# Four load buffers that keep their columns of ones, and a running maximum, in an attention and expert kernel

## The chip, the cores and the metric

The kernel runs on one core of a Trainium2 chip. The metric is the device time of one execution in microseconds (us). The engines are called PE (matrix products; PEld is its weight load), DVE, ACT, POOL and SP; SP issues the plain transfers, POOL the scatters.

## What is computed

```python
B, N, C = (4, 11456, 128); n_agents = 49
def sm(a, b):
    s = scale * (a @ b.transpose(0, 2, 1))
    s = s - s.max(-1, keepdims=True)
    e = np.exp(s)
    return e / (e.sum(-1, keepdims=True) + 1e-09)
a2k = sm(agents, k)
agent_v = a2k @ v
q2a = sm(q, agents)
attn = q2a @ agent_v                 # 4 x 11456 x 128
# then, with the 45824 rows as x, an expert layer with 8 experts:
logits = x @ w_gate
expert_idx = np.argmax(logits, axis=1)
probs = softmax(logits)
h = np.maximum(x_sorted[lo:hi] @ w1[e], 0.0)
y_sorted[lo:hi] = h @ w2[e]          # rows sorted by expert
out = gate_w[:, None] * y
```

The agents look at the keys of their batch with a softmax over 11456 keys, so the maximum and the sum run over all keys. Each query row then looks at 49 agents, is sent to one expert, and is weighted by its gate.

## The kernel before

A batch has 90 blocks of 128 rows. Keys and values are worked off in nine units of ten blocks (UB = 10, 640 KB each); queries in units of eight or ten. For the keys (`k_ops`) a unit is loaded to a buffer of the ring `cf` (L357), ACT rounds it to f16 (`chi`, L361), DVE makes the rest (`clo`, L365), PE forms the scores in PSUM (L380 to L382), ACT copies them to `S` (L425), and DVE takes the maximum of the unit's ten blocks (L430), one column of `mx` for each unit. After the ninth, DVE reduces `mx` (L439), and a short chain over PE, DVE and ACT spreads the maximum `m`. For the values (`v_ops`) POOL first writes a column of ones behind each of the ten blocks of a `cf` buffer (L485), SP loads the ten blocks between them (L488), DVE or POOL subtracts `m` (L491), ACT takes the exponential (L494), and PE sums `S` times `v` and, by the ones, the softmax's denominator (L502). ACT copies the two halves of the sum to `vsum` (L517).

`cf` has four buffers, which keys, values, most of the queries and four of the w2 experts share in turn. A buffer is handed on when its last readers are done.

The expert part sorts a group's rows by expert (`r_ops`, on DVE), scatters them to DRAM with one POOL transfer for each block (`rows`, L951), and reads them back as tiles of 128 rows of one expert. A tile is two layers on PE (L1020 and L1021, then L1027, L1028 and L1033), a relu on ACT (L1069), its f16 rest on DVE (`hlo`, L1073), a scaling on ACT (`yo`, L1084) and a scatter of the rows by POOL (`out`, L951). There are 372 tiles in nine groups; the first group has only 16 blocks, so that tiles begin early. Keys, values and queries of later batches are worked off between tiles. On each engine the order of instructions is fixed when the program is built: a planner (`Plan.run`) simulates the engines with a cost for each step and a key that says when it is due, and emits the steps in the order in which its simulation starts them. A step's cost in the planner thus changes the order of all that comes later.

Of the kernel before, what the change touches and what calls it, by code (L numbers as in the profile page):

```python
# [11 lines left out]
F32 = mybir.dt.float32  # L12
# [12 lines left out]
A = 49  # L25
# [194 lines left out]
def agent_attention_moe(ctx: ExitStack, tc: tile.TileContext, qT, kT, v, agT, wg, w1, w2, out):  # L220
    nc = tc.nc
# [12 lines left out]
    def buf(name, shape, dt=F32, **kw):  # L234
        return wk.tile(shape, dt, name=name, bufs=RINGS.get(name, 1), **kw)
# [56 lines left out]
    PL = Plan()  # L292
# [4 lines left out]
    def dve(n):  # L297
        return 0.07 + 0.00104 * n
# [45 lines left out]
    def dma(src, dst, nbytes, key, deps=(), new=(), use=(), q=None, fn=None):  # L344
        return PL.op("SP", 0.53, fn or (lambda: nc.sync.dma_start(dst(), src())), key, deps,
                     new=new, use=use, nbytes=nbytes)


    def split(src, key, hk, pool=False, ring="cf", ub=UB):

        st = Rec()
        n = ub * P
        gf, gh, gl = Gen(ring), Gen("chi"), Gen("clo")

        def ld():
            st.f = buf(ring, [P, UB * (P + 1)] if ring == "cf" else [P, F])[:, :n]
            nc.sync.dma_start(st.f, src)  # L357

        def hi():
            st.hi = buf("chi", [P, UC], F16)[:, :n]  # L360
            nc.scalar.copy(st.hi, st.f)  # L361

        def lo():
            st.lo = buf("clo", [P, UC], F16)[:, :n]
            (nc.gpsimd if pool else nc.vector).tensor_sub(st.lo, st.f, st.hi)  # L365
        o0 = dma(None, None, P * n * 4, key, new=[gf], fn=ld)
        st.ld = o0
        o1 = PL.op("ACT", 0.03 + act(n), hi, hk, [o0], new=[gh], use=[gf])
        o2 = PL.op("POOL" if pool else "DVE", pol(n) if pool else dve(n), lo, hk, [o1], new=[gl], use=[gf, gh])
        return st, [o1, o2], [gh, gl]  # L370
# [33 lines left out]
    def k_ops(t, key, pool=()):  # L404

        b = t.b
        agents_ops(t, key())
        t.gS, t.gmx = Gen("S"), Gen("mx")
        t.o_s = []

        def begin():
            t.S = buf("S", [P, NBLK, A])
            t.mx = buf("mx", [P, NU, A])
            nc.gpsimd.memset(spacer, 0.0)
        ob = PL.op("POOL", 0.04, begin, key(), new=[t.gS, t.gmx])
        om = []
        for u in range(NU):
            k = key()
            st, sp, gs = split(kT[b][:, u * UC:(u + 1) * UC], k - 1.5, k, pool=u in pool)
            r, o, gm = scores(t, st, sp + [ob], gs, k)  # L420
            t.ga.users.append(o)
            sl = slice(u * UB, (u + 1) * UB)

            def cp(sl=sl, r=r):
                nc.scalar.copy(t.S[:, sl], r.p)  # L425

            def mx(sl=sl, u=u):
                if u == NU - 1:
                    nc.vector.memset(t.S[TAIL:, NBLK - 1], NEG)
                nc.vector.tensor_reduce(t.mx[:, u], t.S[:, sl].rearrange("p k a -> p a k"), axis=AX.X, op=OP.max)  # L430
            o = PL.op("ACT", act(UA), cp, k, [o, ob], use=[gm, t.gS])
            o = PL.op("DVE", 0.9, mx, k, [o], use=[t.gS, t.gmx])
            t.o_s.append(o)
            om.append(o)
        t.gm, g1 = Gen("m"), Gen("m1")

        def red():
            t.m1 = buf("m1", [P, A])
            nc.vector.tensor_reduce(t.m1, t.mx.rearrange("p u a -> p a u"), axis=AX.X, op=OP.max)  # L439


        x = Rec()
        g2, g3, gp, gq = Gen("mt"), Gen("mg"), Gen("misc"), Gen("misc")

        def tr():
            x.p = misc([A, P])
            nc.tensor.transpose(x.p, t.m1, identf)

        def diag():
            x.t = buf("mt", [A, 1])  # L450
            nc.vector.tensor_reduce(x.t, x.p, axis=AX.X, op=OP.max)
            x.d = buf("mg", [A, A])
            nc.vector.tensor_scalar(x.d, identf[:A, :A], x.t, None, op0=OP.mult)

        def every():
            x.q = misc([P, A])
            nc.tensor.matmul(x.q, onesf[:A], x.d, start=True, stop=True)

        def cpm():
            t.m = buf("m", [P, A])  # L460
            nc.scalar.copy(t.m, x.q)
        k = key()
        o = PL.op("DVE", dve(NU * A), red, k, om, new=[g1], use=[t.gmx])
        o = PL.op("PE", 0.25, tr, k, [o], new=[gp], use=[g1])
        o = PL.op("DVE", 0.4, diag, k, [o], new=[g2, g3], use=[gp])
        o = PL.op("PE", 0.25, every, k, [o], new=[gq], use=[g3])
        t.o_m = PL.op("ACT", act(A), cpm, k, [o], new=[t.gm], use=[gq])

    def v_ops(t, key, pool=()):

        b = t.b
# [4 lines left out]
        for u in range(NU):  # L476
            en, ec, ew = ("POOL", pol, nc.gpsimd) if u in pool else ("DVE", dve, nc.vector)
            k = key()
            sl = slice(u * UB, (u + 1) * UB)
            st = Rec()  # L480
            gf = Gen("cf")

            def one(st=st):
                st.f = buf("cf", [P, UB, P + 1])
                nc.gpsimd.memset(st.f[:, :, P:], 1.0)  # L485

            def ld(u=u, st=st):
                nc.sync.dma_start(st.f[:, :, 0:P], v[b][:, u * UC:(u + 1) * UC].rearrange("p (k c) -> p k c", c=P))  # L488

            def sub(sl=sl, ew=ew):  # L490
                ew.tensor_tensor(t.S[:, sl], t.S[:, sl], t.m[:, None, :].to_broadcast([P, UB, A]), op=OP.subtract)  # L491

            def ex(sl=sl):
                nc.scalar.activation(t.S[:, sl], t.S[:, sl], AF.Exp, scale=scale)  # L494

            def mm(u=u, st=st):

                if u == 0:
                    r.v = misc([P, P + 1])
                for j in range(UB):  # L500
                    h = 64 * (j % 2)
                    nc.tensor.matmul(r.v[h:h + A], t.S[:, u * UB + j], st.f[:, j], start=(u == 0 and j < 2),  # L502
                                     stop=(u == NU - 1 and j >= UB - 2))
            o = PL.op("POOL", 0.14, one, k - 1.5, new=[gf])
            ol = dma(None, None, P * UC * 4, k - 1.5, [o], use=[gf], fn=ld)
            t.o_vl.append(ol)
            o = PL.op(en, ec(UA), sub, k, [t.o_m] + t.o_s[u:u + 1], use=[t.gS, t.gm])
            o = PL.op("ACT", act(UA), ex, k, [o], use=[t.gS])
            oM.append(PL.op("PE", UB * 0.087, mm, k, [o, ol] + oM[-1:], new=[] if u else [gv],
                            use=[gf, t.gS] + ([gv] if u else [])))  # L510

# [2 lines left out]
        t.gav, t.gab, t.gan, t.gG, t.gbm = Gen("av"), Gen("ab"), Gen("an"), Gen("G"), Gen("bm")  # L514

        def c0(h):
            nc.scalar.copy(vsum[h:h + A], r.v[h:h + A])  # L517

        def c1():
            r.l = misc([P, 1])  # L520
# [16 lines left out]
            t.ab = buf("ab", [P, A])  # L537
            nc.vector.scalar_tensor_tensor(t.ab, t.av[:, A2:A2 + A], -1.0, t.av[:, A2:A2 + A], op0=OP.mult, op1=OP.max)
        k = key()
        o = [PL.op("ACT", 0.17, lambda h=h: c0(h), k, oM, use=[gv]) for h in (0, 64)]  # L540
        o = PL.op("PE", 0.1, c1, k, o + [o_cst], new=[gm])
        o = PL.op("DVE", 0.5, c1b, k, [o], new=[g1, gs], use=[gm])
        o = PL.op("PE", 0.22, c1c, k, [o], new=[ga], use=[gs])
# [558 lines left out]
    def w_ops(e, lkey, key):  # L1102

        r = Rec()
        ring = "S" if e in W2S else "cf" if e in W2CF else "wf"
        t = BT[0]
        gf = t.gS if ring == "S" else Gen(ring)

        def ld():
            if ring == "S":  # L1110
                i = len(W1S) + W2S.index(e)
                r.f = t.S.rearrange("p k a -> p (k a)")[:, i * F:(i + 1) * F]
            else:
                r.f = buf("cf", [P, UB * (P + 1)])[:, :F] if ring == "cf" else buf("wf", [P, F])
            nc.sync.dma_start(r.f, w2[e])
            r.f = r.f.rearrange("p (k d) -> p k d", d=P)

        def hi():
            m = w2s[:, e].rearrange("p (k i d) -> p k i d", i=2, d=P)
            r.hi, r.lo = m[:, :, 0], m[:, :, 1]  # L1120
            nc.scalar.activation(r.hi, r.f, AF.Copy, scale=SW)

        def lo():
            nc.vector.scalar_tensor_tensor(r.lo, r.f, SW, r.hi, op0=OP.mult, op1=OP.subtract)

# [137 lines left out]
```

## Time and profile before

| | |
|---|---|
| time, median of 3 runs | 1520.91 us (1517.16 to 1523.62) |
| the profiled execution: its time, its span | 1521.53 us, 1519.7 us |
| busy: PE, DVE, POOL, ACT | 1180.8, 860.7, 834.2, 753.3 us |
| mean busy share of the 16 DMA engines on SP's queue | 37.9% |

The span is the time from the first to the last instruction; the rest of the 1521.53 us lies around it. A busy PE counts pipelined matmuls, so it isn't PE at its peak.

### The profile page before, as it was taken

To read this page: it belongs to the slowest core of one execution; us is meant where nothing else is said; L and a number is where in the kernel's file an instruction comes from. 1 tells how busy PE (TensorE), PEld (TensorE's weight loads), DVE (VectorE), ACT (ScalarE), POOL (GpSimd) and SP (SyncE) were. 2 spreads that over 40 slices of the span, in tenths; PEclk is the share of its full clock that TensorE was granted. 3 is DMA by queue.
4 is the path that set the end of the run, shared out by engine and by line. 5 is a ranking of instruction groups with operands and counts; after the bars stand their busy time and mean duration, and the time that the engine had idled before them with its cause. 6 is when DMAs were issued, how large, how long until landed. Compare 5 with 4: busy or idle time off the path is not lost. (4 is left out here: it accounts for less than half of the span.)

```text
span 1519.7 us, 46051 instructions
## 1 busy us (share of the span) xinstructions
PE 1180.8 (78%) x18670; PEld 1066.0 (70%) x18670; DVE 860.7 (57%) x1273; ACT 753.3 (50%) x1162; POOL 834.2 (55%) x1537
## 2 busy tenths in 40 slices
PE   4743767778877798888777788888787887879995
PEld 3442666567777786767777786777777776779995
DVE  7674675367657646574557754568447433334553
ACT  5552734354644545554554544646454443435663
POOL 1156355655556656566556755556556555664443
PEclk9866778999889998999899989999999999999998
DMA  8988435764174377264252639346131123132220
GB/s 281 322 281 237 129 97 165 203 214 105 29 220 121 109 189 224 69 176 134 60 177 71 179 83 287 87 120 152 38 100 40 41 78 108 41 66 71 49 47 23
DMA packets 222099, 198.40 MB, mean 131 GB/s; under 512 B 121123, under 2 KB 189869, under 8 KB 221857
## 3 DMA queue, kind: packets, MB, share of 16 engines
q1 hardware_dynamic: 198432, 162.15, 37.9%
q0 software_dynamic: 23424, 33.05, 7.7%
q8 instruction: 149, 2.44, 0.7%
q14 instruction: 94, 0.76, 0.2%
HBM read 107.98 MB, written 59.60 MB: 110 GB/s over the span
## 5 line engine op out<-in xcount | busy, mean ns | idle before, releaser
L1073 DVE SCALAR_TENSOR_TENSOR hlo<-hp,hhi 128x1024 f16<-128x1024 f32 x372 | 452.8, 1222 | 448.3 <-ACT hhi L1069 403.0
L951 POOL DMA_INDIRECT out<-yo,rt x372 | 388.8, 1045 | 501.2 <-ACT yo L1084 470.1
L1069 ACT ACTIVATE hhi<-hp 128x1024 f16<-128x1024 f32 x372 | 380.8, 1024 | 253.5 <-PE hp L1021 115.8
L1027 PE MATMUL yp<-Wst,hhi 128*128 128x128 f16 x2976 | 394.3, 225 | 118.8 <-ACT yo L1084 96.5
L951 POOL DMA_INDIRECT rows<-rows,idx x360 | 376.8, 1047 | 118.4 <-issue 82.5
L1020 PE MATMUL hp<-ec,Mst 98*128 98x128 f16 x2976 | 407.4, 226 | 29.4 <-issue 16.5
L1021 PE MATMUL hp<-ec,Mst 98*128 98x128 f16 x2976 | 405.1, 226 | 16.6 <-issue 15.9
L1028 PE MATMUL yp<-Wst,hhi 128*128 128x128 f16 x2976 | 394.3, 225 | 3.7 <-issue 3.7
L1028 PEld LDWEIGHTS <-hhi 128*128 128x128 f16 x2976 | 300.4, 101 | 131.7 <-issue 130.6
L1020 PEld LDWEIGHTS <-Mst 98*128 98x128 f16 x2976 | 300.7, 101 | 40.4 <-issue 31.1
L1021 PEld LDWEIGHTS <-Mst 98*128 98x128 f16 x2976 | 301.6, 102 | 28.7 <-issue 27.9
L1027 PEld LDWEIGHTS <-hhi 128*128 128x128 f16 x2976 | 299.8, 101 | 23.7 <-issue 15.7
L1084 ACT ACTIVATE yo<-yp,rt 128x128 f32<-128x128 f32 x372 | 137.0, 368 | 301.3 <-PE hp L1021 175.4
L1033 PE MATMUL yp<-Wst,hlo 128*128 128x128 f16 x2976 | 246.0, 226 | 28.3 <-issue 15.4
L1033 PEld LDWEIGHTS <-hlo 128*128 128x128 f16 x2976 | 191.0, 102 | 47.3 <-issue 25.2
L382 PE MATMUL misc<-a,clo 128*128 128x49 f16 x720 | 79.1, 194 | 42.7 <-issue 26.3
L365 DVE TENSOR_TENSOR clo<-cf,chi 128x1280 f16<-128x1280 f32 (+1 forms) x71 | 104.6, 1473 | 10.4 <-ACT chi L361 6.5
L361 ACT CAST chi<-cf 128x1280 f16<-128x1280 f32 (+1 forms) x71 | 88.7, 1251 | 35.4 <-remote 13.2
L380 PE MATMUL misc<-a,chi 128*128 128x49 f16 x720 | 78.7, 194 | 32.5 <-ACT chi L361 18.8
L382 PEld LDWEIGHTS <-clo 128*128 128x128 f16 x720 | 65.5, 103 | 43.0 <-issue 25.0
L380 PEld LDWEIGHTS <-chi 128*128 128x128 f16 x720 | 66.6, 103 | 40.1 <-ACT chi L361 19.9
L381 PE MATMUL misc<-a,chi 128*128 128x49 f16 x720 | 78.8, 195 | 14.7 <-issue 14.6
(173 smaller groups left out, 955.7 us busy)
## 6 DMA issues: line engine op xcount, KB each, us to landing
cf<-in_kT SPq DMA_DIRECT2D x36, 640.0 KB
cf<-in_v SPq DMA_DIRECT2D x36, 640.0 KB
cf<-in_qT SPq DMA_DIRECT2D x32, 640.0 KB
Mst<-md SPq DMA_DIRECT2D x30, 512.0 KB
Wst<-w2s SPq DMA_DIRECT2D x30, 512.0 KB
wf<-in_w SPq DMA_DIRECT2D x28, 512.0 KB
rows<-padrow SPq DMA_DIRECT2D x4, 2304.0 KB
md<-mm SPq DMA_DIRECT2D x56, 128.0 KB
```

The source lines that it names most:

```text
L365: (nc.gpsimd if pool else nc.vector).tensor_sub(st.lo, st.f, st.hi)
L380: nc.tensor.matmul(p[:, j], h, t.a[:, 0], start=True, stop=False)
L382: nc.tensor.matmul(p[:, j], l, t.a[:, 0], start=False, stop=True)
L951: st = nc.gpsimd.indirect_dma_start(out=dst, out_offset=bass.IndirectOffsetOnAxis(ap=idx, axis=0), in_=src, in_offset=None, **kw)
L1020: nc.tensor.matmul(h_, m[:A2, h, c:c + P], e, start=True, stop=False)
L1021: nc.tensor.matmul(h_, m[:A2, h, 512 + c:512 + c + P], e, start=False, stop=True)
L1027: nc.tensor.matmul(yp, h, w[:, fb * 256 + P:(fb + 1) * 256], start=(fb == 0), stop=False)
L1028: nc.tensor.matmul(yp, h, w[:, fb * 256:fb * 256 + P], start=False, stop=False)
L1033: nc.tensor.matmul(yp, lo[:, fb * P:(fb + 1) * P], w[:, fb * 256:fb * 256 + P], start=False, stop=(fb == FB - 1))
L1069: nc.scalar.activation(x.hi, x.hp, AF.Relu)
L1073: nc.vector.scalar_tensor_tensor(x.lo, x.hp, 0.0, x.hi, op0=OP.max, op1=OP.subtract)
L1084: nc.scalar.activation(x.yo, x.yp, AF.Copy, scale=r.rt[:, o, 1:2].bitcast(F32))
```

## The change

Four buffers `CF` are now made once, with columns of ones that are written at the start and never again: a column of ones, then two blocks of 128, then a column of ones, and so on. The first block of a pair has its ones on its left, the second on its right. All loads to `cf` (keys, values, queries, w2) go between the columns, in pieces of two blocks: 1024 bytes. Before, those of v were pieces of 512 bytes, and those of keys and queries 5120 (4096 for units of eight blocks and for w2). The nine POOL writes of ones for each batch are gone. For the maximum, DVE keeps a running maximum of 128x490 over the units (nothing for the first unit, the first against the second for the second), and the last reduce takes the ten blocks of it. The copy of the first half of the sum is two ACT instructions, since its ones stand on the other side.

```diff
+    PW = 2 * P + 1
+    CF = [cst.tile([P, UB // 2 * PW + 1], F32, name=f"cf{i}") for i in range(RINGS["cf"])]
+    for t in CF:
+        nc.gpsimd.memset(t[:, 0::PW], 1.0)
+    cf_n = [0]
+
+    def cfbuf():
+        cf_n[0] += 1
+        return CF[(cf_n[0] - 1) % len(CF)]
+
+    def pairs(t, n):
+
+        return t[:, 1:1 + n // 2 * PW].rearrange("p (s c) -> p s c", c=PW)[:, :, 0:2 * P]
...
-            st.f = buf(ring, [P, UB * (P + 1)] if ring == "cf" else [P, F])[:, :n]
-            nc.sync.dma_start(st.f, src)
+            st.f = pairs(cfbuf(), ub) if ring == "cf" else by_pairs(buf(ring, [P, F])[:, :n])
+            nc.sync.dma_start(st.f, by_pairs(src))
...
-            t.mx = buf("mx", [P, NU, A])
+            t.mx = buf("mx", [P, UB, A])
...
-                nc.vector.tensor_reduce(t.mx[:, u], t.S[:, sl].rearrange("p k a -> p a k"), axis=AX.X, op=OP.max)
+                nc.vector.tensor_tensor(t.mx, t.S[:, 0:UB] if u == 1 else t.mx, t.S[:, sl], op=OP.max)
             o = PL.op("ACT", act(UA), cp, k, [o, ob], use=[gm, t.gS])
-            o = PL.op("DVE", 0.9, mx, k, [o], use=[t.gS, t.gmx])
+            if u:
+                o = PL.op("DVE", dve(UA), mx, k, [o] + t.o_s[-1:], use=[t.gS, t.gmx])
...
-            def one(st=st):
-                st.f = buf("cf", [P, UB, P + 1])
-                nc.gpsimd.memset(st.f[:, :, P:], 1.0)
-
             def ld(u=u, st=st):
-                nc.sync.dma_start(st.f[:, :, 0:P], v[b][:, u * UC:(u + 1) * UC].rearrange("p (k c) -> p k c", c=P))
+                st.f = cfbuf()
+                nc.sync.dma_start(pairs(st.f, UB), by_pairs(v[b][:, u * UC:(u + 1) * UC]))
...
-            o = PL.op("POOL", 0.14, one, k - 1.5, new=[gf])
-            ol = dma(None, None, P * UC * 4, k - 1.5, [o], use=[gf], fn=ld)
+            ol = dma(None, None, P * UC * 4, k - 1.5, new=[gf], fn=ld)
...
-            nc.scalar.copy(vsum[h:h + A], r.v[h:h + A])
+            if h:
+                nc.scalar.copy(vsum[h:h + A], r.v[h:h + A])
+            else:
+                nc.scalar.copy(vsum[0:A, P:], r.v[0:A, 0:1])
+                nc.scalar.copy(vsum[0:A, 0:P], r.v[0:A, 1:])
```

On SP, the loads of v for the first batch (L488) stood so, with the semaphores that each waits for:

```order
L488 DMA cf<-in_v 128x10x128 [waits DMAHW0_49,DVE_49]
L488 DMA cf<-in_v 128x10x128 [waits DMAHW1_49,DVE_49]
L488 DMA cf<-in_v 128x10x128 [waits DMAHW2_49,DVE_49]
L357 DMA wf<-in_qT 128x1024 x2
L488 DMA cf<-in_v 128x10x128 [waits DMAHW3_49,PE_49,Pool_49]
L488 DMA cf<-in_v 128x10x128 [waits DMAHW5_49,PE_49,Pool_49]
L488 DMA cf<-in_v 128x10x128 [waits DMAHW4_49,DMAHW6_49,PE_49,Pool_49]
L488 DMA cf<-in_v 128x10x128 [waits DMAHW7_49,PE_49,Pool_49]
L488 DMA cf<-in_v 128x10x128 [waits DMAHW2_49,PE_49,Pool_49]
```

With the change the same loads are L505, and stand in the same order:

```order
L505 DMA cf_111<-in_v 128x5x256 [waits DMAHW0_49,DVE_49]
L505 DMA cf_112<-in_v 128x5x256 [waits DMAHW1_49,DVE_49]
L505 DMA cf_109<-in_v 128x5x256 [waits DMAHW2_49,DVE_49]
L376 DMA wf<-in_qT 128x1024 x2
L505 DMA cf_110<-in_v 128x5x256 [waits DMAHW3_49,PE_49]
L505 DMA cf_111<-in_v 128x5x256 [waits DMAHW5_49,PE_49]
L505 DMA cf_112<-in_v 128x5x256 [waits DMAHW6_49,DMAHW4_49,PE_49]
L505 DMA cf_109<-in_v 128x5x256 [waits DMAHW7_49,PE_49]
L505 DMA cf_110<-in_v 128x5x256 [waits DMAHW2_49,PE_49]
```

Nothing moved here; the last five no longer wait for POOL, only for PE, which frees the buffer. In exchange the first four loads of keys, which waited for nothing, now wait for POOL's writes of ones.

On DVE, where the keys of the second batch begin among the first tiles (L365 is `clo`, L1073 `hlo` of a tile, L430 the maximum, L723 and L724 belong to the queries), the rows were:

```order
L687 TENSOR_TENSOR rows<-ef,rows 128x10x49
L1073 SCALAR_TENSOR_TENSOR hlo<-hp,hhi 128x1024
L365 TENSOR_TENSOR clo<-cf,chi 128x1280
L1002 UNCONDITIONAL_BRANCH
L1073 SCALAR_TENSOR_TENSOR hlo<-hp,hhi 128x1024
L430 TENSOR_REDUCE mx<-S 128x49
L1002 UNCONDITIONAL_BRANCH
L365 TENSOR_TENSOR clo<-cf,chi 128x1280
L723 TENSOR_TENSOR lg<-ls 128x80
```

Now they are (L384 for L365, L1094 for L1073):

```order
L708 TENSOR_TENSOR rows<-ef,rows 128x10x49
L1094 SCALAR_TENSOR_TENSOR hlo<-hp,hhi 128x1024
L384 TENSOR_TENSOR clo<-cf_112,chi 128x1280
L1023 UNCONDITIONAL_BRANCH
L1094 SCALAR_TENSOR_TENSOR hlo<-hp,hhi 128x1024
L1023 UNCONDITIONAL_BRANCH
L384 TENSOR_TENSOR clo<-cf_109,chi 128x1280
L744 TENSOR_TENSOR lg<-ls 128x80
```

The maximum of the first unit has gone from this place; the next one stands behind the sorting of a group's rows in both.

On DVE again, the keys of the third batch (units two to five) were spread among tiles so:

```order
L1073 SCALAR_TENSOR_TENSOR hlo<-hp,hhi 128x1024 x2
L430 TENSOR_REDUCE mx<-S 128x49
L1002 UNCONDITIONAL_BRANCH
L365 TENSOR_TENSOR clo<-cf,chi 128x1280
L1002 UNCONDITIONAL_BRANCH
L1073 SCALAR_TENSOR_TENSOR hlo<-hp,hhi 128x1024 x2
L430 TENSOR_REDUCE mx<-S 128x49
L1002 UNCONDITIONAL_BRANCH
L365 TENSOR_TENSOR clo<-cf,chi 128x1280
L1002 UNCONDITIONAL_BRANCH
L1073 SCALAR_TENSOR_TENSOR hlo<-hp,hhi 128x1024 x2
```

Now the maxima of the second to fourth unit (L449) stand so:

```order
L449 TENSOR_TENSOR mx<-S 128x490
L384 TENSOR_TENSOR clo<-cf_109,chi 128x1280
L449 TENSOR_TENSOR mx<-mx,S 128x490
L1094 SCALAR_TENSOR_TENSOR hlo<-hp,hhi 128x1024
L1023 UNCONDITIONAL_BRANCH
L384 TENSOR_TENSOR clo<-cf_110,chi 128x1280
L449 TENSOR_TENSOR mx<-mx,S 128x490
L1094 SCALAR_TENSOR_TENSOR hlo<-hp,hhi 128x1024
L1023 UNCONDITIONAL_BRANCH
L1094 SCALAR_TENSOR_TENSOR hlo<-hp,hhi 128x1024
L449 TENSOR_TENSOR mx<-mx,S 128x490
```

Counted by the rows of L1073, the nine maxima of this batch lay between the 72nd and the 85th tile, and the eight lie now between the 79th and the 86th; those of the last batch lay between the 158th and the 173rd, and lie now between the 164th and the 177th.

## Rows read from the trace of the kernel before

**Rows 1.** Busy time by engine in two stretches, then clock, DMA share, GB/s.

```profile
0.00:160.00 160.00, 75.20 (x1027) 59.52 (x1028) 100.54 (x216) 69.41 (x105) 63.72 (x121) 0.77 0.84 267
160.00:1368.00 1208.00, 971.72 (x15272) 873.51 (x15271) 687.56 (x997) 601.33 (x938) 704.81 (x1292) 0.94 0.45 123
```

**Rows 2.** Waits over the whole run: us in total, times, longest.

```profile
PE yp L1027 <- ACT yo L1084: 96.5, 117, 3.1
...
POOL cf L485 <- PE misc L502: 13.9, 8, 5.0
...
PE yp L1033 <- DVE hlo L1073: 12.7, 10, 6.2
...
ACT chi L361 <- DMA cf<-in_qT: 6.7, 4, 3.4
...
PE misc L502 <- DMA cf<-in_v: 5.0, 6, 1.4
```

**Rows 3.** Timeline, PE, first batch's values: start, length, count, idle before.

```profile
35.42 7.35 PE L502 MATMUL misc<-cf,S 128*49 128x129 f32 x80 [1.69 <-issue]
...
44.03 1.31 PE L502 MATMUL misc<-cf,S 128*49 128x129 f32 x20
...
53.35 1.31 PE L502 MATMUL misc<-cf,S 128*49 128x129 f32 x20 [1.09 <-DMA cf<-in_v]
```

**Rows 4.** Timeline, SP and POOL, around the fifth and ninth load of v.

```profile
37.88 0.38 SPq L488 DMA_DIRECT2D cf<-in_v  x1
...
45.42 1.92 SPq L488 DMA_DIRECT2D cf<-in_v  x1
...
34.05 4.61 POOL L491 TENSOR_TENSOR S<-S,m 128x490 f32<-128x490 f32 x3 [6.25 <-ACT m L461]
38.61 0.11 POOL L485 MEMSET cf<- 128x10 f32 x1
```

**Rows 5.** As rows 1, while v is loaded and while w1 and w2 are.

```profile
40.00:50.00 10.00, 7.69 (x147) 7.01 (x144) 6.40 (x8) 4.58 (x9) 2.12 (x6) 1.00 0.97 265
56.00:66.00 10.00, 6.08 (x42) 2.89 (x43) 6.83 (x36) 4.00 (x10) 0.00 (x0) 0.61 1.02 413
```

**Rows 6.** Timeline, SP and POOL, the first microseconds.

```profile
1.69 1.38 SPq L357 DMA_DIRECT2D cf<-in_kT  x3
...
2.50 0.10 POOL L414 MEMSET spacer<- 1x1 f32 x1
```

**Rows 7.** Timeline, ACT and DVE, the first batch's keys.

```profile
6.07 1.26 ACT L361 CAST chi<-cf 128x1280 f16<-128x1280 f32 x1 [3.36 <-DMA cf<-in_kT]
...
19.68 0.57 ACT L425 COPY S<-misc 128x490 f32<-128x490 f32 x1 [0.67 <-PE misc L382]
...
16.75 1.49 DVE L365 TENSOR_TENSOR clo<-cf,chi 128x1280 f16<-128x1280 f32 x1
...
21.44 1.49 DVE L365 TENSOR_TENSOR clo<-cf,chi 128x1280 f16<-128x1280 f32 x1
...
30.85 0.94 DVE L439 TENSOR_REDUCE m<-mx 128x49 f32<-128x441 f32 x1
```

**Rows 8.** Groups by line and shape: busy us, mean ns of one, idle before.

```profile
L430 DVE TENSOR_REDUCE mx<-S 128x49 f32<-128x490 f32 x36 | 35.8, 997 | 29.7 <-ACT S L425 25.0 <-issue 3.1 <-ACT hhi L1069 1.5
...
L491 DVE TENSOR_TENSOR S<-S,m 128x490 f32<-128x490 f32 x32 | 22.0, 749 | 2.2 <-ACT m L461 2.1
...
L517 ACT COPY vsum<-misc 49x129 f32<-49x129 f32 x8 | 2.1, 263 | 11.2 <-PE misc L502 8.8 <-PE yp L1033 2.4
```

**Rows 9.** DVE's timeline, then PE's waits between 171 and 216 us.

```profile
178.80 1.02 DVE L430 TENSOR_REDUCE mx<-S 128x49 f32<-128x490 f32 x1
...
PE yp L1033 <- DVE hlo L1073: 8.9, 3, 6.2
```

**Rows 10.** Busy time of L1084 (ACT, once a tile) in two stretches.

```profile
477.00:531.00 54.00, 4.81 (x13) 0.95 0.45 129
1254.00:1368.00 114.00, 12.45 (x34) 1.00 0.30 72
```

More of the change, by code (lines that the diff above doesn't have):

```diff
@@ L281, in agent_attention_moe, with by_pairs @@
     nc.vector.memset(vsum, 0.0)
+    PW = 2 * P + 1
[8 more added lines that the diff above has]
+        return t[:, 1:1 + n // 2 * PW].rearrange("p (s c) -> p s c", c=PW)[:, :, 0:2 * P]
+    def by_pairs(x):
+        return x.rearrange("p (s c) -> p s c", c=2 * P)
     w2s = cst.tile([P, NE, FB * 256], F16, name="w2s")
@@ L355, in ld @@
         def ld():
-            st.f = buf(ring, [P, UB * (P + 1)] if ring == "cf" else [P, F])[:, :n]
-            nc.sync.dma_start(st.f, src)
+            st.f = pairs(cfbuf(), ub) if ring == "cf" else by_pairs(buf(ring, [P, F])[:, :n])
+            nc.sync.dma_start(st.f, by_pairs(src))
         def hi():
             st.hi = buf("chi", [P, UC], F16)[:, :n]
-            nc.scalar.copy(st.hi, st.f)
+            nc.scalar.copy(by_pairs(st.hi), st.f)
         def lo():
             st.lo = buf("clo", [P, UC], F16)[:, :n]
-            (nc.gpsimd if pool else nc.vector).tensor_sub(st.lo, st.f, st.hi)
+            (nc.gpsimd if pool else nc.vector).tensor_sub(by_pairs(st.lo), st.f, by_pairs(st.hi))
         o0 = dma(None, None, P * n * 4, key, new=[gf], fn=ld)
@@ L462, in k_ops @@
         k = key()
-        o = PL.op("DVE", dve(NU * A), red, k, om, new=[g1], use=[t.gmx])
+        o = PL.op("DVE", 0.9, red, k, om, new=[g1], use=[t.gmx])
         o = PL.op("PE", 0.25, tr, k, [o], new=[gp], use=[g1])
@@ L501, in mm @@
                     h = 64 * (j % 2)
-                    nc.tensor.matmul(r.v[h:h + A], t.S[:, u * UB + j], st.f[:, j], start=(u == 0 and j < 2),
+                    c = j // 2 * PW + j % 2 * (P + 1)
+                    nc.tensor.matmul(r.v[h:h + A], t.S[:, u * UB + j], st.f[:, c:c + P + 1], start=(u == 0 and j < 2),
                                      stop=(u == NU - 1 and j >= UB - 2))
-            o = PL.op("POOL", 0.14, one, k - 1.5, new=[gf])
-            ol = dma(None, None, P * UC * 4, k - 1.5, [o], use=[gf], fn=ld)
+            ol = dma(None, None, P * UC * 4, k - 1.5, new=[gf], fn=ld)
             t.o_vl.append(ol)
@@ L539, in v_ops @@
         k = key()
-        o = [PL.op("ACT", 0.17, lambda h=h: c0(h), k, oM, use=[gv]) for h in (0, 64)]
+        o = [PL.op("ACT", 0.17 if h else 0.25, lambda h=h: c0(h), k, oM, use=[gv]) for h in (0, 64)]
         o = PL.op("PE", 0.1, c1, k, o + [o_cst], new=[gm])
@@ L1113, in ld @@
             else:
-                r.f = buf("cf", [P, UB * (P + 1)])[:, :F] if ring == "cf" else buf("wf", [P, F])
-            nc.sync.dma_start(r.f, w2[e])
-            r.f = r.f.rearrange("p (k d) -> p k d", d=P)
+                r.f = pairs(cfbuf(), FB) if ring == "cf" else buf("wf", [P, F])
+            if ring != "cf":
+                r.f = by_pairs(r.f)
+            nc.sync.dma_start(r.f, by_pairs(w2[e]))
+            r.f = r.f.rearrange("p s (h d) -> p s h d", d=P)
         def hi():
-            m = w2s[:, e].rearrange("p (k i d) -> p k i d", i=2, d=P)
-            r.hi, r.lo = m[:, :, 0], m[:, :, 1]
+            m = w2s[:, e].rearrange("p (s h i d) -> p s h i d", h=2, i=2, d=P)
+            r.hi, r.lo = m[:, :, :, 0], m[:, :, :, 1]
             nc.scalar.activation(r.hi, r.f, AF.Copy, scale=SW)
```

## The prediction, made before the changed kernel ran

> **What bounds the kernel now.** I read the busy times by stretch first, since one share over the run mixes two programs. Until 160 us the engines wait for data and for one another: PE is busy for 75 of 160 us and the DMA engines for 0.84 of the time. From 160 to 1368 us PE is busy for 972 of 1208 us, the DMA for 0.45 [rows 1]. So transfers can set the end only in the first stretch. Nearly everything there is one chain: keys, maximum, values, sorting, scatter, first tile. All engines work in a fixed order, so what the chain gains before the first tile moves the rest along. Next the waits over the run: behind the first stretch PE waits above all for ACT's `yo` (96.5 us), which the change leaves alone. For DVE's `hlo` it waits 12.7 us, for v 5.0 us. POOL waits 13.9 us at the ones of v for PE, but no row of these waits shows PE waiting for POOL [rows 2]. Last the timelines, for when each step of the first batch runs [rows 3, 4, 6, 7].
>
> **The change, part by part.** The sum is made against the profiled execution, 1521.5 us, of which 1519.7 are the span; the median of the runs is 1520.9, so I predict about 0.6 us high if that execution was no better than another.
>
> Price of a piece. The v loads move 265 GB/s at a DMA share of 0.97; w1 and w2, in pieces of 4096 bytes, 413 GB/s at 1.02 [rows 5]. For each of 16 engines that is 30.9 ns for 512 bytes and 158.7 ns for 4096. A straight line between them is 12.6 ns for each piece and 0.0357 ns for each byte, so 49.2 ns for 1024 bytes and 195 ns for 5120. A load of 640 KB (655,360 bytes) takes by this estimate 2.47 us in pieces of 512, 1.97 in 1024, 1.56 in 5120. Each v load gains 0.50 us, each load of keys or queries loses 0.41. There are 36 of the first and about 71 of the second, so the transfers as a whole grow by some 11 us; what counts is which of them somebody waits for.
>
> The Trainium skill, "DMA: Bandwidth & Descriptors", Specifications, gives 512 bytes as the smallest transfer for line rate. By that rule larger pieces give v nothing, and the sum below would end at 1520.6. The rows at 265 and 413 GB/s disagree with it.
>
> Keys of the first batch. Their first load was issued at 1.69 us and waited for nothing. Now it waits for POOL's first column of ones, which stands ahead of the write at 2.50 us [rows 6]; so it goes at about 2.65, 0.95 later, and takes 0.41 longer. Then two units take 4.69 us (21.44 less 16.75). DVE fills them with two `clo` and two maxima, but another chain is as long: `clo`, PE's scores, ACT's copy at 19.68, `chi`, `clo` of the unit after next [rows 7]. A shorter maximum therefore frees DVE and not the stage. Only the last maximum counts: 997 ns as a reduction; the nearest row for the new form is the subtraction of 128x490 in f32, 749 ns [rows 8], so I take 0.3 less (at least nothing, at most 0.4). The last reduction, 0.94 us [rows 7], reads 490 for 441 elements and grows by at most 0.1, which I leave inside that. Values begin 0.95 + 0.41 - 0.3 = 1.06 us later.
>
> Values of the first batch. SP's fifth load was issued at 37.88 us, behind POOL's write of ones, which stood behind 4.61 us of POOL's subtractions [rows 4]. Without POOL it needs only the first unit's products: 80 matmuls took 7.35 us, so a unit 1.84 [rows 3], and 35.42 + 1.06 + 1.84 is 38.3 us. No gain there. The ninth load needs the fifth unit's products, 44.03 to 45.34 before, so it goes at 46.4 for 45.42 [rows 3, 4]. But it was used only at 53.35, 7.9 us after its issue, because five loads of 2.47 us stood in a row. Four loads of 1.97 us from 38.3 are through at 46.2, so it now finds the queue nearly empty. It then takes at least its 1.97 us (48.4) and at most what the first load of keys took from issue to use, 6.07 - 1.69 = 4.38 [rows 6, 7], and 0.41 more (51.2). I take 50.75, nearer to the whole latency: the last products start 2.6 us earlier. If the pieces aren't quicker it is 0.4 later instead. The sum's first half takes three ACT copies for two, 263 ns each [rows 8]: 0.26 back. From here to the first tile nothing else is changed: -2.3 us.
>
> Second batch. Between 171 and 216 us PE waits 8.9 us for DVE's `hlo`. The maximum at 178.80, 1.02 us, stands between two `hlo` there and is gone [rows 9]: -1.0 us (nothing, if `hlo` then waits for ACT). The other 23 or so maxima beyond the first batch are about 0.25 us shorter each, but PE's waits for `hlo` outside this place are 12.7 - 8.9 = 3.8 us in all [rows 2, 9]. I take a quarter of them, -1.0 (0 to -3.8).
>
> The Trainium skill, "VectorE: DVE Perf Modes", in its tier table, has f32 `tensor_tensor` and `tensor_reduce` both at one element a cycle, so by it the new maximum saves nothing where 490 elements stay 490. The sum would lose these 2.0 us and end at 1519.6. The rows differ from it: 997 ns with the reduction's strided read against 749.
>
> Longer loads of queries and keys. ACT waits 6.7 us for queries, four times [rows 2]. Four times 0.41 is 1.6; a load that others wait for still hides part of it, so I take a quarter, +0.4 (0 to +1.6). The waits of POOL at the ones, gone now, I cost at nothing: POOL is busy for 705 of 1208 us [rows 1], so its scatters have room; if that cover is thin, the second rival holds.
>
> Sum: -2.6 + 0.26 - 1.0 - 1.0 + 0.4 = -3.9, so **1517.6 us**.
>
> **Rivals.** *The start gains nothing.* Pieces of 1024 bytes are as slow as those of 512, or the scatter and the w loads behind it take the gain: +0.4 + 0.26 - 1.0 - 1.0 + 0.4 = -0.9, 1520.6 us. For it speaks that w1 and w2 queue right behind v at a DMA share of 1.02; against it the difference of 265 and 413 GB/s [rows 5].
>
> *The later batches gain too.* POOL stood still for 13.9 us at the ones, up to 5.0 at once [rows 2], with scatters of rows and outputs queued behind, and SP's loads of v behind POOL. If half of that reaches the tiles, 7 us, it comes to 1510.6 us. Against it: PE's waits for v are 5.0 us in the whole run, the first batch included [rows 2].
>
> *Slower: the third batch's keys crowd.* The planner now starts nine units between the 78th and the 86th tile, which spread over 13 tiles before. There 13 tiles took 54 us, against 34 in 114, so 3.35 each, where nothing else runs [rows 10]: nine units cost 54 - 13 x 3.35 = 10.4 us, 1.16 each. If that price stays, crowding is free, since five tiles are relieved. If a unit costs what it does alone in the first batch, 4.69 / 2 = 2.35, it is 9 x 1.19 = 10.7 us more: 1528.3 us. It decides from 3.9 / 9 = 0.43 us a unit. For it: `clo` and the maximum of a unit now stand between every two `hlo`. Against it: DVE is busy for only 688 of 1208 us behind the first stretch [rows 1].
>
> **How the numbers follow.** The forecast has 0.42, no gain at the start 0.15, the later batches 0.25, the crowd 0.18. The forecast's own range is 1512 to 1521, by the ends of its terms (48.4 and 53.8 for the last v, 0 and -3.8 for `hlo`, +1.6 for queries). The range that leaves 2 in 10 out is 1506 to 1529. A difference of 0.5% (7.6 us) is about what a measurement of this kernel can tell from none. Below 1513.3 lie most of the later-batches case (0.23) and a quarter of the forecast (0.11): faster 0.34. Above 1528.5 lies about half of the crowd and some of what a new order may do elsewhere: slower 0.14. The rest, 0.52, is no difference.
>
> **What would show it.** The first load of keys issued near 2.6 us; two units of keys still in about 4.7 us; v at 333 GB/s, and the last products of the first batch starting near 50.7; the first tile's layer 2 to 2.5 us earlier; maxima of 0.65 to 0.75 us; 13 tiles and nine units of the third batch still in about 54 us from the 72nd tile on. It is wrong if v's loads stay at 2.4 us, if the 24 later maxima take 1 us, or if tiles from the 78th to the 86th take over 5 us each.

## The result, and the profile after

The change took 1498.95 us (median of 4 runs, 1497.77 to 1502.17) beside 1520.86 for the kernel before: a ratio of 0.9877, with a 95% interval from 0.9842 to 0.9913. The forecast was 1517.6. The profiled execution has a span of 1500.3 us (1519.7 before) and a mean granted clock of 0.931 (0.921).

First the start, which the forecast had down for most of the gain. Timelines of the change, SP, POOL, DVE, PE and ACT (columns as in [rows 3]):

```profile
2.51 0.21 POOL L287 MEMSET cf<- 128x6 f32 x4
...
30.98 0.67 DVE L449 TENSOR_TENSOR mx<-mx,S 128x490 f32<-128x490 f32 x1
31.69 0.97 DVE L459 TENSOR_REDUCE m<-mx 128x49 f32<-128x490 f32 x1
...
36.28 6.70 PE L520 MATMUL misc<-cf,S 128*49 128x129 f32 x80 [1.69 <-ACT S L511]
...
38.71 0.38 SPq L505 DMA_DIRECT2D cf<-in_v  x1
...
44.98 0.37 SPq L505 DMA_DIRECT2D cf<-in_v  x1
...
53.73 1.31 PE L520 MATMUL misc<-cf,S 128*49 128x129 f32 x20 [0.56 <-DMA cf<-in_v]
...
107.75 0.37 ACT L1105 ACTIVATE yo<-yp,rt 128x128 f32<-128x128 f32 x1
```

The products of v begin at 36.28 us for 35.42, the last of them at 53.73 for 53.35 [rows 3], and the first tile's `yo` at 107.75 for 107.27. So the start gave nothing. Why shows in the windows of the change (columns as in [rows 1]):

```profile
38.00:40.00 2.00, 2.00 (x23) 2.00 (x21) 2.00 (x3) 1.94 (x3) 2.00 (x3) 1.00 0.15 17
40.00:42.00 2.00, 2.00 (x34) 2.00 (x32) 2.00 (x3) 2.00 (x4) 1.09 (x2) 1.00 0.86 280
42.00:44.00 2.00, 2.00 (x49) 1.77 (x47) 2.00 (x3) 1.10 (x3) 0.00 (x0) 1.00 0.88 207
...
46.00:50.00 4.00, 1.31 (x21) 1.12 (x21) 1.98 (x4) 1.36 (x3) 0.00 (x0) 1.00 1.07 355
```

The larger pieces are quicker: 355 GB/s from 46 to 50 us where the engines are full, against 265 before [rows 5]. By the trace's packets only v moves in these 4 us, and a piece of 1024 bytes takes 50 ns (49.2 in the forecast). The Trainium skill, "DMA: Bandwidth & Descriptors", Specifications, has line rate from 512 bytes on; these rows disagree. But the transfer engines stand nearly still from 38 to 40 us and are not full until 44: PE frees the buffers one by one, and the fifth to eighth load were issued at 38.71, 40.81, 41.91 and 43.01 us. Counted by the packets, the eighth was through at about 49.0 us, not at 46.2. The ninth, issued at 44.98, was used 8.75 us later: its last 68 of 640 pieces came after 51 us, the last at 53.1, among some 90 pieces a us of the w loads.

Then the two stretches of [rows 1], the second up to the same tile:

```profile
0.00:160.00 160.00, 73.68 (x1020) 58.54 (x1021) 96.69 (x214) 68.82 (x106) 61.03 (x116) 0.78 0.86 267
160.00:1348.00 1188.00, 958.10 (x15265) 856.16 (x15265) 675.39 (x994) 601.47 (x941) 705.68 (x1263) 0.95 0.45 125
```

The first has nearly the same PE work, 1020 matmuls for 1027. The second does as many matmuls as before (15265 for 15272) in 1188 us for 1208, 14 us of it less PE time and the rest less idle time. The waits of the whole run that answer to [rows 2], and the new maximum:

```profile
PE yp L1048 <- ACT yo L1105: 91.9, 115, 2.4
...
PE yp L1054 <- DVE hlo L1094: 10.5, 6, 6.2
...
ACT chi L380 <- DMA cf<-in_qT: 7.2, 3, 4.2
...
PE misc L520 <- DMA cf<-in_v: 1.7, 3, 0.6
...
L449 DVE TENSOR_TENSOR mx<-mx,S 128x490 f32<-128x490 f32 x28 | 18.7, 669 | 21.8 <-ACT S L444 21.1 <-DVE clo L384 0.4
```

No wait of PE has shrunk by anything like 20 us. POOL's 13.9 us at the ones are gone, PE's wait for `yo` is 4.6 us shorter. Where the time went shows when each tile's `yo` (L1084, now L1105) is set against the same tile of before, from the rows of ACT's timeline:

```
tile              0      12      18      24      36      54      60      78      90     108     180     371
before us    107.27  203.92  234.97  267.37  345.37  418.40  443.46  510.35  563.45  643.44  914.97 1504.38
change less   +0.48   +1.52   -8.05   -2.79  -12.22  -11.86  -18.27  -21.21  -14.55  -18.86  -19.72  -19.07
```

All of the gain arises between the 12th and the 78th tile, while the second batch and the first keys of the third are worked off. Behind them it goes up and down and ends where it was.

### The profile page after: what moved, and what is told of

Read it like the earlier page. It is cut to its first block, busy times and chain, and to the rows that moved or that the text cites. A ratio compares the mean times of both kernels' runs of the same rounds, so it can differ in the third digit from the quotient of the medians.

```text
span 1500.3 us, 45968 instructions
## 1 busy us (share of the span) xinstructions
PE 1166.5 (78%) x18670; PEld 1048.5 (70%) x18670; DVE 845.5 (56%) x1269; ACT 752.8 (50%) x1166; POOL 832.9 (56%) x1505
## 5 line engine op out<-in xcount | busy, mean ns | idle before, releaser
L1094 DVE SCALAR_TENSOR_TENSOR hlo<-hp,hhi 128x1024 f16<-128x1024 f32 x372 | 452.9, 1221 | 441.9 <-ACT hhi L1090 380.8
L972 POOL DMA_INDIRECT out<-yo,rt x372 | 384.6, 1034 | 492.7 <-ACT yo L1105 451.5
L1090 ACT ACTIVATE hhi<-hp 128x1024 f16<-128x1024 f32 x372 | 381.0, 1024 | 240.6 <-PE hp L1042 99.0
L1048 PE MATMUL yp<-Wst,hhi 128*128 128x128 f16 x2976 | 392.7, 224 | 115.2 <-ACT yo L1105 91.9
L972 POOL DMA_INDIRECT rows<-rows,idx x360 | 382.8, 1063 | 124.4 <-issue 84.6
L1041 PE MATMUL hp<-ec,Mst 98*128 98x128 f16 x2976 | 397.4, 223 | 33.0 <-issue 25.3
L1042 PE MATMUL hp<-ec,Mst 98*128 98x128 f16 x2976 | 396.0, 223 | 15.7 <-issue 15.6
L1041 PEld LDWEIGHTS <-Mst 98*128 98x128 f16 x2976 | 296.1, 100 | 49.1 <-issue 40.5
L1042 PEld LDWEIGHTS <-Mst 98*128 98x128 f16 x2976 | 297.5, 100 | 26.5 <-issue 26.1
L1048 PEld LDWEIGHTS <-hhi 128*128 128x128 f16 x2976 | 298.4, 101 | 24.8 <-issue 14.6
L1105 ACT ACTIVATE yo<-yp,rt 128x128 f32<-128x128 f32 x372 | 137.0, 368 | 296.7 <-PE hp L1042 167.0
L384 DVE TENSOR_TENSOR clo<-cf,chi 128x1280 f16<-128x1280 f32 (+1 forms) x71 | 104.6, 1474 | 21.0 <-ACT chi L380 18.0
L399 PE MATMUL misc<-a,chi 128*128 128x49 f16 x720 | 76.4, 193 | 30.8 <-ACT chi L380 20.8
L400 PE MATMUL misc<-a,chi 128*128 128x49 f16 x720 | 76.5, 193 | 16.5 <-issue 16.3
```

What stands on the lines that cost most here:

```text
L384: (nc.gpsimd if pool else nc.vector).tensor_sub(by_pairs(st.lo), st.f, by_pairs(st.hi))
L399: nc.tensor.matmul(p[:, j], h, t.a[:, 0], start=True, stop=False)
L972: st = nc.gpsimd.indirect_dma_start(out=dst, out_offset=bass.IndirectOffsetOnAxis(ap=idx, axis=0), in_=src, in_offset=None, **kw)
L1041: nc.tensor.matmul(h_, m[:A2, h, c:c + P], e, start=True, stop=False)
L1042: nc.tensor.matmul(h_, m[:A2, h, 512 + c:512 + c + P], e, start=False, stop=True)
L1048: nc.tensor.matmul(yp, h, w[:, fb * 256 + P:(fb + 1) * 256], start=(fb == 0), stop=False)
```

## The experiments

Two theories. **Order**: the planner was told other costs (none for the ones, 0.58 for 0.90 of a maximum), and the order it made of them is better, whatever the instructions are. **Work**: the instructions themselves are cheaper (no waits of POOL, larger pieces, lighter maxima). Each ratio below is to runs of the kernel before on the same chip, with its 95% interval.

**Instructions and order crossed.** The first kernel has the change's instructions in the order of before, the second the instructions of before in the change's order (the main lines; the planner's costs of the last reduction and of the sum's copies are exchanged too):

```diff
 # e1, from the change
-            if u:
-                o = PL.op("DVE", dve(UA), mx, k, [o] + t.o_s[-1:], use=[t.gS, t.gmx])
+            o = PL.op("DVE", 0.9, mx, k, [o], use=[t.gS, t.gmx])   # emits nothing for u == 0
+            o = PL.op("POOL", 0.14, one, k - 1.5, new=[gf])        # takes the buffer, emits nothing
 # e2, from before
-            o = PL.op("POOL", 0.14, one, k - 1.5, new=[gf])        # the memset goes into ld
-            o = PL.op("DVE", 0.9, mx, k, [o], use=[t.gS, t.gmx])
+            if u:                                                  # u == 1 emits two reductions
+                o = PL.op("DVE", dve(UA), mx, k, [o] + t.o_s[-1:], use=[t.gS, t.gmx])
```

> All instructions of the change (fixed buffers, pairs, running maximum), but planned with the costs of before, so that every engine keeps the order of before. Theory 1 (the 22 us came from the planner's new order, and the new instructions themselves are worth a few us at most): 1515 to 1521 us. Theory 2 (the instructions gave it: POOL no longer stands 13.9 us at the ones, v comes in larger pieces, the maxima are lighter): 1497 to 1503 us.

> The instructions of before (ones written by POOL for each unit of v, pieces of 512 and 5120 bytes, reductions of 0.997 us), planned with the costs of the change, so that every engine has the order of the change. Theory 1 (order): 1498 to 1506 us. Theory 2 (instructions): 1517 to 1523 us.

The first gave 1511.37 us, 0.9953 (0.9915 to 0.9991); the second 1505.46, 0.9875 (0.9809 to 0.9941), in four runs. Neither theory holds alone, and most of the gain goes with the order.

**Each half of the change, with its costs.**

> Before with the running maximum alone, costs in the planner included. Theory 1 (order) gives no sign: the order is a third one, and the time can lie anywhere from 1498 to 1530 us. Theory 2 (instructions): lighter maxima alone are worth some 2 us, 1517 to 1520 us, if POOL's waits and the pieces gave the rest; 1499 to 1503 us if the maxima gave it all.

> The change without the running maximum: fixed buffers and pieces of 1024 bytes, reductions as before, planned at their old cost. Theory 1 (order) gives no sign: 1498 to 1530 us. Theory 2 with POOL's waits and the pieces as the source: 1500 to 1505 us; with the maxima as the source: 1517 to 1522 us.

0.9943 (0.9911 to 0.9976) and 0.9964 (0.9940 to 0.9988). Both halves gain, 0.6% and 0.4%, together 0.9% beside 1.2% for the whole. Their times, 1512.8 and 1512.5 us, lie in none of the ranges of Theory 2; by themselves they don't say whether work or order gains.

**Is an order a draw?** One cost nudged by 0.02 moves hundreds of rows:

```diff
-            o = PL.op("DVE", 0.9, mx, ...)             # before
+            o = PL.op("DVE", 0.88, mx, ...)            # e5; 0.92 in e6
-                o = PL.op("DVE", dve(UA), mx, ...)     # the change
+                o = PL.op("DVE", dve(UA) - 0.02, mx, ...)   # e7; + 0.02 in e8
```

> Before, with nothing changed but the planner's cost of a maximum, 0.88 for 0.90; the instructions are the same, some hundreds of rows stand in another order. Theory A (an order is a draw: any nudge moves the time by several us either way): somewhere in 1505 to 1530 us, off 1520 by over 5 us in at least two of the four nudges of this set. Theory B (the change's order is better for a reason that lies in what it removes, and a nudge changes little): 1517 to 1523 us.

> Before, with the planner's cost of a maximum 0.92 for 0.90. Theory A: 1505 to 1530 us. Theory B: 1517 to 1523 us.

> The change, with the planner's cost of a running maximum 0.02 less. Theory A: 1490 to 1520 us. Theory B: 1496 to 1502 us.

> The change, with the planner's cost of a running maximum 0.02 more. Theory A: 1490 to 1520 us; if the mean of the two nudged changes is above 1508 us, the change's 1499 us was a good draw. Theory B: 1496 to 1502 us.

On that chip before takes 1541 us. The nudged kernels of before gave 0.9989 (0.9960 to 1.0017) and 1.0027 (0.9996 to 1.0058), the nudged changes 0.9907 (0.9878 to 0.9936) and 0.9933 (0.9900 to 0.9967). Of the time of before, 1520.9 us, that is 1519.2, 1525.0, 1506.7 and 1510.7 us. Theory B fits the first and misses the second by 2 us; the nudged changes lie outside its range, and their mean of 1508.7 is just above the 1508 from which on the change's own 1499 was to count as a good draw. So a nudge is worth some 0.3%, and the change's orders stay ahead.

**The work alone, in the old order.** e9 has only the running maximum's instructions, e11 only the fixed buffers, e12 does the maxima of the later batches twice, e10 is e11 with each load of v in two halves:

```diff
 # e12, from before
+                for _ in range(2 if b else 1):
                     nc.vector.tensor_reduce(t.mx[:, u], ...)
 # e10, from e11
-                nc.sync.dma_start(pairs(st.f, UB), by_pairs(v[b][:, u * UC:(u + 1) * UC]))
+                src = by_pairs(v[b][:, u * UC:(u + 1) * UC])
+                for c in (0, P):
+                    nc.sync.dma_start(pairs(st.f, UB)[:, :, c:c + P], src[:, :, c:c + P])
```

> Before with the running maximum's instructions alone, planned at the old costs, so that every other row stands where it stood. DVE loses some 11 us of work behind the first batch (3 maxima gone, 24 shorter by 0.33 us). Theory 1 (DVE's time counts although PE is seen to wait only 12.7 us for it): ratio 0.995 to 0.997, 5 to 8 us. Theory 2 (hidden beside the tiles, the gain came from the new order alone): 0.998 to 1.000.

> Before with fixed buffers, old maxima, old order, and each load of v as two transfers in pieces of 512 bytes: POOL's writes of ones and its 13.9 us of waits are gone, the pieces of v stay as they were (keys and queries in 1024 bytes). Theory 1 (POOL's standing still held back scatters and loads): ratio 0.995 to 0.997. Theory 2 (the larger pieces of v are what the fixed buffers give): 0.999 to 1.002.

> As the run without POOL's waits, but v in pieces of 1024 bytes, one transfer a unit. Theory 1 (POOL's waits): the same ratio as that run within 0.002. Theory 2 (pieces): 0.995 to 0.997, and that run at 0.999 to 1.002.

> Before with each maximum of the second to fourth batch done twice: 27 x 1.0 = 27 us more work for DVE, nothing else moved. Theory 1 (DVE's time counts at about half its length): ratio 1.007 to 1.010. Theory 2 (hidden): 1.000 to 1.003.

e9: 0.9983 (0.9951 to 1.0014), as Theory 2 had it. e12: 1.0001 (0.9965 to 1.0038), though its DVE works 62.6 us at maxima instead of 35.8:

```profile
L431 DVE TENSOR_REDUCE mx<-S 128x49 f32<-128x490 f32 x63 | 62.6, 995 | 21.1 <-ACT S L425 15.5 <-issue 4.5
```

So behind the first batch the maxima are hidden. e11: 0.9970 (0.9938 to 1.0002), at most a small gain. e10 can't part the two theories: 1.0255 (1.0204 to 1.0305), because in it SP holds the second half of a buffer back until the first has landed. SP's waits in e10:

```profile
SPq L508 <- DMA cf<-in_v: 103.5, 29, 6.5
```

What POOL's waits and the pieces are each worth stays open. One thing can be read from e10: nine of these waits, 36.2 us, lie in the first batch, and its first tile comes 19.6 us later than before; the other 20, 67.3 us, add only some 15 us by the profiles, 20 by the medians.

**The old work in four more orders of the change's costs.** These are the orders of e7, e8, e3 and e4, with the instructions of before:

> The instructions of before in the order of the nudged change (its maximum planned 0.02 shorter; with the new instructions that order gave 0.9907). Theory 1 (the order that the changed costs give is worth the gain, whatever the instructions): 0.989 to 0.994. Theory 2 (the instructions are worth it, and 0.9875 for the old instructions in the change's own order was a good draw): 0.998 to 1.003. Half and half: 0.995.

> The instructions of before in the order of the other nudged change (0.02 longer; 0.9933 with the new instructions). Theory 1: 0.991 to 0.996. Theory 2: 0.998 to 1.003.

> The instructions of before, planned with the changed costs of the maxima alone (0.58 for 0.90, none for the first unit, 0.90 for the last reduction): the order of the run with the running maximum alone, which gave 0.9943. Theory 1: 0.992 to 0.996. Theory 2: 0.998 to 1.003.

> The instructions of before, planned without a step for the writes of ones (they are emitted with the load of v): the order of the run with fixed buffers alone, which gave 0.9964. Theory 1: 0.994 to 0.998. Theory 2: 0.998 to 1.003.

They gave 0.9921 (0.9885 to 0.9957), 0.9958 (0.9927 to 0.9988), 0.9974 (0.9946 to 1.0002) and 0.9983 (0.9954 to 1.0011): the first two as Theory 1 had it, the third between the two, the last as Theory 2. All ratios by order:

```
order made of                     work of before       work of the change
costs of before                   1                    0.9953
the change's costs                0.9875 (4 runs)      0.9877
the same, maximum 0.02 less       0.9921               0.9907
the same, maximum 0.02 more       0.9958               0.9933
costs of the maxima alone         0.9974               0.9943 (running maximum only)
cost of the ones alone            0.9983               0.9964 (fixed buffers only)
```

The mean of the three orders of the change's costs is 0.9918 with the old work and 0.9906 with the new. The order gives about 0.8% (12 us) by the left column and 0.5% (7 us) by the right. The work gives 0.1% to 0.5% (2 to 7 us), and some 0.3% is the draw of the change's own order, which the old work shows too (0.9875). Each ratio is known to within 0.2% to 0.7% only: that the change's orders gain is clear, how the rest divides is not.

**Where the order gains.** Lengths in us between tiles, mean and extremes of the profiles of seven kernels in the order of before or nudged from it (before, e1, e5, e6, e9, e11, e12) and of six in the change's (change, e2, e7, e8, e13, e14):

```
tiles      old order             the change's order
12-24      65.9 (63.4 to 69.7)   60.2 (59.0 to 62.1)
24-56     156.8 (151.3 to 163.9) 153.8 (148.4 to 158.6)
56-72      59.9 (58.0 to 63.6)   55.5 (52.8 to 60.6)
72-90      76.4 (73.3 to 78.3)   81.4 (77.6 to 86.7)
90-108     82.1 (78.3 to 89.8)   76.7 (73.6 to 79.7)
```

The tiles from 12 to 24 hold the second batch's last keys and its values, those from 24 to 56 its queries, the others the third batch. Work moved from the 56th to 72nd and the 90th to 108th tile to those between; these lose 5.0 us and the others win 9.8. From the 12th to the 24th tile the ranges don't touch. Two kernels in that stretch, e9 (old order) and then e13 (the change's order):

```profile
208.41:275.07 66.66, 52.05 (x767) 47.26 (x766) 34.42 (x39) 28.36 (x45) 37.79 (x70) 0.81 0.58 142
```

```profile
205.23:264.81 59.58, 49.60 (x813) 44.76 (x811) 38.27 (x41) 28.11 (x45) 38.17 (x73) 0.91 0.63 163
```

In e13 PE does 46 matmuls more in 7 us less. Over the thirteen profiles its waits there are 14.6 us in the old order and 10.9 in the new (for `yo` 3.8 and 2.3, for `hlo` 1.4 and 0.0), and the granted clock is 0.82 and 0.91. So the new order lets PE pause less there, and more of the stretch runs at the higher of the clock's two levels, 2.4 GHz.

From the 12th to the 108th tile as a whole PE waits hardly less, and the clock is what differs. Before, then the change:

```profile
203.92:643.44 439.52, 352.50 (x5379) 311.15 (x5377) 257.63 (x377) 219.32 (x344) 261.06 (x475) 0.90 0.53 149
```

```profile
205.44:624.58 419.14, 338.97 (x5386) 298.51 (x5385) 250.22 (x374) 218.14 (x345) 262.63 (x452) 0.93 0.53 154
```

By the thirteen profiles this stretch takes 441.1 us in the old order and 427.6 in the new. PE's waits in it are 87.3 us (78.5 to 101.1) and 84.7 (78.0 to 89.0), the time at the lower level of the clock, 1.2 GHz, is 89.4 us (81.4 to 99.0) and 63.0 (51.2 to 68.3): these ranges don't touch, whichever instructions a kernel has. Work that takes 26.4 us at the lower level takes half at the higher, so that the clock could give most of the 13.5 us; this is an estimate, and what in the order keeps the clock up is not shown. Over the whole run the clock doesn't explain the ratios: e2 has 0.9245 beside 0.9246 of before, and 0.9875 of its time.

**The start.** e17 puts the w loads behind the last products of v, e18 writes the ones first:

```diff
 # e17
-        o.after = [vl[n]]
+        o.after = [vl[n]] + [x for x in BT[0].o_ml[7:] if x is not o]   # w1[7] first, to the end of S
...
 # e18: these lines moved ahead of all other POOL work
+    CF = [cst.tile([P, UB // 2 * PW + 1], F32, name=f"cf{i}") for i in range(RINGS["cf"])]
+    for t in CF:
+        nc.gpsimd.memset(t[:, 0::PW], 1.0)
```

> The change, with the loads of w1 and w2 behind the last products of v: the first of them goes to the end of S, which those products still read, and SP takes the others after it. Theory S1 (the w loads, issued right behind v's ninth load, take a share of the transfer engines and hold back its last pieces; that ate the forecast 2.6 us): the last products of the first batch start at 51.3 to 52.2 us. Theory S2 (v's own loads and their landing set it): 52.5 to 53.8 as in the other runs of the change. Either way the w loads come 7 us later, and the first scatter and the first tile some 5 us later than in the change.

> The change, with the columns of ones written as POOL's first work, so that the first load of keys waits for nothing again. Keys issued at 1.7 us for 2.65, the maximum m spread at 33.7 to 33.9 us (34.64 in the change), the first products of v at 35.4. If the chain carries on, the first tile is up to 0.9 us earlier; if the transfers of the rows set it, not. In total 1497 to 1501 us, ratio 0.985 to 0.990: no difference from the change that can be told, unless its own ratio was a good draw (then 0.990 to 0.993).

In e17 the transfers of v are over sooner, the last piece at 52.2 us for 53.1, and then PE loses it again. Windows of e17:

```profile
50.00:52.00 2.00, 1.49 (x22) 1.26 (x19) 0.00 (x0) 0.00 (x0) 0.00 (x0) 0.82 0.41 138
52.00:54.00 2.00, 2.00 (x23) 2.00 (x21) 0.00 (x0) 0.00 (x0) 0.00 (x0) 0.50 0.06 13
```

The DMA share falls to 0.41 and 0.06: nine of the 640 pieces of the ninth load came after 52 us. But the eighth unit's products, from 51.11 on, run into a granted clock of 0.50 (1.2 GHz) after a stretch of short products and waits, and the last unit starts near 53. Neither theory is shown. The first tile comes 4.9 us later than in the change, as expected, the first scatter of rows does not (71.82 us for 71.67). e18 does what it should at the start: keys issued at 1.69, last products at 51.54, and that with the w loads right behind v. Its first scatter of rows begins at 69.57 us, 1.92 earlier than before, but its first `yo` at 107.03 only 0.24 earlier: what the start gains is lost between the scatters and the first tile.

These two ran on a chip on which the kernel before takes 1191 us (seven runs, 1188 to 1194), not 1517 to 1541 as on those of the other experiments. On it e18 is **slower** than before, 1205.34 us, 1.0115 (1.0075 to 1.0155), where 0.985 to 0.990 was expected; e17's one run took 1205.63. Some of PE's waits in the whole of e18, the longest first:

```profile
PE misc L402 <- DVE clo L385: 20.2, 15, 7.1
PE yp L1055 <- DVE hlo L1095: 17.6, 17, 6.6
...
PE yp L1049 <- ACT yo L1106: 8.6, 9, 2.4
...
PE misc L521 <- issue: 1.7, 1, 1.7
...
PE yp L1050 <- issue: 0.3, 1, 0.3
```

In the change PE waits 91.9 us for `yo`, and 133 us in 288 pieces between 107 and 1500 us at "issue", for nothing that the profile shows. Here that is 8.6 and 0.3. All matmuls between the first tile and the last stretch, the change's profile and then e18's:

```profile
107.00:1392.00 1285.00, 1020.04 (x16285) 914.61 (x16282) 723.91 (x1081) 641.14 (x1000) 758.63 (x1360) 0.94 0.46 127
```

```profile
107.00:1095.00 988.00, 908.88 (x16262) 867.33 (x16260) 714.47 (x1080) 648.49 (x998) 765.02 (x1360) 0.97 0.61 165
```

The same 16,300 matmuls take 1285 us there and 988 here. The change itself was not timed on this chip; e18 differs from it only in the place of four writes on POOL. Nor were order and work parted here, so which of them loses is not shown.

Where PE pauses can be read further. Before, while POOL still scatters rows beside the tiles and then behind the last of these scatters (1371.08 us); then e18, while they still run:

```profile
1254.00:1368.00 114.00, 88.92 (x1376) 78.99 (x1374) 41.98 (x35) 44.54 (x68) 68.55 (x133) 1.00 0.30 72
1376.00:1505.00 129.00, 127.79 (x2281) 127.37 (x2278) 70.32 (x60) 78.95 (x115) 60.53 (x116) 1.00 0.23 52
```

```profile
1000.00:1060.00 60.00, 60.00 (x1077) 60.00 (x1075) 33.07 (x27) 37.18 (x55) 48.20 (x93) 1.00 0.28 70
```

The clock is 1.00 in all three. PE is idle for 25 of 114 us while rows are scattered, for 1 of 129 behind, and in e18 not at all, though a scatter takes 0.96 us on both chips. In the change the last scatter of rows begins at 1351.9 us, and behind 1356.3 PE waits once more, for 0.5 us at the end. So on the slower chips the pauses go with the scatters of rows; whether these cause them is not shown.

## Why the prediction was wrong, by its own steps

- **Keys, +1.06.** Right: first load issued at 2.65 us (forecast 2.65), last maximum 0.67 us long for 0.98, two units still in 4.69, values 0.86 later.
- **Values of the first batch, -2.6.** Wrong by 3. The price of a piece was right. The step that failed is "Four loads of 1.97 us from 38.3 are through at 46.2, so it now finds the queue nearly empty": PE hands the buffers on one at a time, the transfer engines stand at a share of 0.15 from 38 to 40 us, and the ninth load waits behind three others. Without the w loads behind it (e17) v was through 0.9 us sooner, on another chip; the rest stays open. And "From here to the first tile nothing else is changed" would not have held either: in e18 the last products come 1.81 us sooner than before and the first `yo` 0.24.
- **Third copy of the sum, +0.26.** It cost 0.04: the three end 0.58 us after the first begins, the two did after 0.54.
- **Second batch's maximum, -1.0, and the other maxima, -1.0.** Both about nothing. PE waits 8.9 us for `hlo` between 171 and 216 us as in [rows 9], with the maximum between two `hlo` gone. e9 gives 0.9983 with 1 in its interval, e12 1.0001. The new maximum takes 669 ns as forecast (0.65 to 0.75). The Trainium skill, "VectorE: DVE Perf Modes", tier table, has both forms alike; the rows differ by a third, but nothing waits for it.
- **Queries, +0.4.** 7.2 us for 6.7.
- **The sum of the work, -3.9 us.** In the old order all the new work gave 0.9953, 7 us with an interval from 1 to 13. That the size is about right is luck: the start and the maxima, which were to give it, gave nothing, and where the 7 us come from is not shown.
- **The order.** This is the step that made the prediction wrong. It let a new order in only as a loss: in a rival ("The planner now starts nine units between the 78th and the 86th tile") and in the chances ("some of what a new order may do elsewhere: slower 0.14"). Crowding was free, as the rival allowed: from the 72nd `yo`, 13 tiles took 53.8 us, 53.7 before. But no term asked what the places gain that a changed plan leaves, though the text on the planner said that a cost changes the order of all that comes later. The runs showed 7 to 12 us for it, from the 12th to the 108th tile, and a good draw of some 0.3% (5 us).
- **The rival that the later batches gain** had the right place and the wrong reason: POOL's waits and the pieces together (e11) are worth 0.3% with 1 just inside the interval.
- **Two readings.** The price of a tile "where nothing else runs", 3.35 us, comes from a stretch in which POOL still scatters rows; behind the last of them the final 41 tiles take 91.5 us, 2.23 each. Scatters run beside the third batch's keys too, so the price of a unit may stand; but 1.1 us of each tile are a pause that no row of the prediction asked about. And the upper end of the forecast's own range, 53.8 for the last v and +1.6 for queries, adds up to 1523 us, not 1521.

## What to carry to other kernels

Where a planner makes the order, price a changed cost apart from the changed work: run the old instructions under the new costs and the new under the old, and nudge one cost to see what a draw is worth, before the gain is put down to the instructions. A gain at the head of a chain is only real if the step behind it has room: look at when its buffers come free, not only at how fast its transfers are. And a gain measured on some chips need not hold on another: where PE's pauses are gone, the change with its ones written first lost 1.2%.

## What the runs showed of the hardware that was not expected

- The same program took 1520, 1541, 1517, 1521 and 1191 us on five chips. On the last PE's pauses at "issue" are gone (133 us in the change to 0.3 in e18), while a 128x1024 `hlo` takes 1220 ns on both and the last 41 tiles take 91.4 us for 91.5. Why is open.
- Where PE pauses, its work also ends later than its rows say. In the change, from 300 to 1200 us, an ACT that waits begins `yo` 1.2 to 1.4 us (medians of three stretches) behind the recorded end of the tile's last matmul when a scatter of rows falls between 1 us before that matmul and 0.5 us behind it, and 0.04 to 0.10 when none does; in e18 it is 0.04 either way. So much of the 91.9 us that PE waits for `yo` is PE's own delay, not ACT's.
- After PE had waited 0.80, 1.33 and 0.51 us before three units of v in a row, the granted clock stood at 0.50 from 52 to 54 us in e17, although PE was busy throughout those 2 us.
